# An attention, MLP and MoE kernel: attention units in another order, fewer weight tiles converted ahead of the MLP

## The chip, the cores and the metric

The kernel runs on one core of a Trainium2 chip. A core has TensorE (PE, matmul), VectorE (DVE), ScalarE (ACT), GpSimd (POOL) and SyncE (SP, which issues DMAs). Each engine works through its own instructions in the order in which the program lists them, and waits on semaphores for the others. The time is that of one execution on the device, in microseconds (us). The median of three runs of the kernel before is 1107.69 us (1107.59 to 1109.96).

## The reference

Three stages in a row, all in float32 (in outline):

```python
# 1: recurrent attention, 4 batches x 8 heads x 768 steps, head width 48
state = alpha[:, :, t, :, None] * state + einsum('bhd,bhe->bhde', k[:, :, t], v[:, :, t])
y[:, :, t] = einsum('bhd,bhde->bhe', q[:, :, t], state)
# 2: MLP on x = y as [3072 tokens, 384]; w_in [384, 2048], w_out [2048, 384]
h = x @ w_in;  g = h * sigmoid(h);  x = g @ w_out
# 3: noisy top-2 mixture of 8 experts, each 384 -> 1024 -> 384 with relu
logits = x @ w_gate + log1p(exp(x @ w_noise)) * noise;  two best experts per token
out[token] += weight * (relu(x @ w1[e]) @ w2[e])
```

The weights of the MLP come in as 64-bit floats and are used as float32 in two parts, a high part h and a rest l.

## The kernel before

**Attention** is cut into 24 chunks of 128 steps (6 for each batch). For a chunk c, `prep_a`, `prep_b` and `prep_c` make running products of alpha (two scans on DVE, P and R), q times P (POOL, L221), and k times R (DVE, L230). Then come the units on PE: `unit_kt` transposes k (copied to SBUF by ACT as kts), `unit_a` multiplies k with q (16 matmuls), DVE masks the product (`am`, L258), `unit_kv` multiplies kts with v, DVE makes the next state S from it (L277, L278), `unit_y` makes y from S and the masked product in two halves, ACT copies y out as xr, and `unit_x` transposes it to the layout that the MLP reads; ACT and DVE make its high part xh and its rest xl (L310, L311). Three chunks make a token block of 384.

**The MLP** takes 8 blocks, each in 16 steps m. In a step `l1` makes 128 rows of h in nine matmuls (three for each third of the width: two parts of x, two of w_in). `act1` makes the tanh (ACT, L484), gf (DVE, L487), its high part gh (ACT, L492) and the rest gl (DVE, L494). `l2` of two steps earlier adds nine matmuls of g with w_out to three accumulators (L504).

**Weight conversion.** `conv` turns one of the 32 weight tiles (16 of w_in, "i", and 16 of w_out, "o") into its two parts. Three DVE instructions (`narrow`, L148 to L150) make a float32 tile f from the 64-bit words; ACT writes h (L383); POOL issues a DMA that adds h onto f in SBUF (L386, the accumulate); ACT writes l from what is left (L387). A tile of w_out also goes through `fold`: PE transposes f three times (L94), ACT copies that (ft, L394), and `product` multiplies it with the gate's weights (L399), so that the gate's columns come out of `l2` as well; those 16 columns are split too (L401 to L403). f turns over a ring of six buffers (wf and row in the profile are its two tiles), the raw words over three (wraw): the load of a tile is issued on SP once the tile three before it has been narrowed.

**What sets the order.** The program is in the order in which it is written; nothing reorders it. `later(n, fn)` puts a piece of work off until n calls of `tick` have passed. Here it is used for the parts of `conv`, and, in the prologue and in block 0, for am, S and xl as well, one tick later. `stage1_units` hands out attention units one at a time, five to a chunk. The prologue runs 16 of them with nine conversions between them, three chunks in all and the head (`unit_kt`, `unit_a`) of the fourth; block 0 then runs one unit and two conversions in each step until the 32 tiles are through, the first conversion and a tick ahead of the step's tanh, the second after it. From block 1 on nothing is put off.

Of the kernel before, what the change touches and what calls it, by code (L numbers as in the profile page):

```python
# [8 lines left out]
F32 = mybir.dt.float32  # L9
# [43 lines left out]
def attention_mlp_moe(ctx: ExitStack, tc: tile.TileContext, aqk, vt, win, wout, wgn, noise, w12,  # L53
# [175 lines left out]
        k = aqk_t[c][2]  # L229
        DVE.tensor_tensor(k, k, R[:, :, 1:], OP.mult)  # L230

    def bank(c, name, n):
        if c < CPB:
            return pa.tile([128, 512], F32, name=name)[:, :n]
        return p1.tile([128, 512], F32, name="ps1")[:, :n]

    def unit_kt(c):
        t = aqk_t[c]
        if c % NCB < NCB - 1:
            p = bank(c, "acc0", NP * PR).rearrange("p (a b) -> p a b", a=NP)  # L240
            for i in range(NP):
                flip(p[:, i], t[2][:, i])
            k = s1.tile([C, NP, PR], F32, name="kts")
            KTs[c] = k
            ACT.activation(k, p, AF.Copy)

    def unit_a(c):
        t = aqk_t[c]
        p = [p1.tile([C, NP, C], F32, name="ps1") for _ in range(2)]
        for pr in range(NP):  # L250
            for s in range(2):
                PE.matmul(p[s][:, pr], t[2][s * 64:s * 64 + D, pr], t[1][s * 64:s * 64 + D, pr],  # L252
                          start=True, stop=True)

        def am():
            for s in range(2):
                a = s1.tile([C, NP, C], F32, name="am", bufs=3)
                DVE.tensor_tensor(a, p[s], mask_b, OP.mult)  # L258
                AM[c, s] = a

        later(1, am)

    def unit_kv(c):
        if c % NCB == NCB - 1:
            return
        p = p1.tile([PR, NP, 2 * D], F32, name="ps1")
        k = KTs.pop(c)
        for i in range(NP):
            PE.matmul(p[:, i], k[:, i], v_t[c][:, 2 * i:2 * i + 2], start=True, stop=True)
        def state():  # L270
            s = s1.tile([PR, NP, 2 * D], F32, name="S")
            pcm = pcm_t.pop(c)
            if c % NCB == 0:
                DVE.tensor_tensor(s, p, pcm, OP.mult)
            else:
                tmp = s1.tile([PR, NP, 2 * D], F32, name="St", bufs=1)
                DVE.tensor_tensor(tmp, p, Sst[c - 1], OP.add)  # L277
                DVE.tensor_tensor(s, tmp, pcm, OP.mult)  # L278
            Sst[c] = s

        later(1, state)

    def unit_y(c, g):
        t = aqk_t[c]
        if g == 0:
            y_t[c] = bank(c, "acc1", DM).rearrange("p (a b) -> p a b", a=H)
        y = y_t[c]
        for pr in (2 * g, 2 * g + 1):
            f = c % NCB == 0
            if not f:  # L290
                PE.matmul(y[:, 2 * pr:2 * pr + 2], t[1][:, pr], Sst[c - 1][:, pr],
                          start=True, stop=False)
            for s in range(2):
                h = 2 * pr + s
                PE.matmul(y[:, h], AM[c, s][:, pr], v_t[c][:, h], start=f, stop=f or s == 1)  # L295
        if g == 1:
            x = s1.tile([C, KD, 128], F32, name="xr", bufs=1)
            ACT.activation(x.rearrange("p a b -> p (a b)"), y.rearrange("p a b -> p (a b)"), AF.Copy)
            y_t[c] = x

    def unit_x(c):
        j, cc = divmod(c, CPB)
        if cc == 0:
            XH[j], XL[j] = x_tiles(BT)
        x = y_t.pop(c)
        p = bank(c, "acc2", DM).rearrange("p (a b) -> p a b", a=KD)
        for k in range(KD):
            flip(p[:, k], x[:, k])
        sl = slice(cc * C, (cc + 1) * C)
        ACT.activation(XH[j][:, :, sl], p, AF.Copy)  # L310
        later(1, lambda: DVE.tensor_sub(XL[j][:, :, sl], p, XH[j][:, :, sl].bitcast(F32)))  # L311

    dq, lazy, clock = [], [True], [0]

    def later(n, fn, pe=0):
        if lazy[0]:
            dq.append((clock[0] + n, pe, fn))
        else:
            fn()

# [4 lines left out]
        for *_, fn in sorted(due, key=lambda x: x[1]):  # L325
            fn()

    def head(c):
        unit_kt(c)
        unit_a(c)  # L330

    def stage1_units():
        head(0)
        yield
        for c in range(NCH):
            nx = c + 1
            if nx + 1 < NCH and nx + 1 > 2:
                load_chunk(nx + 1)
            if nx < NCH:
                prep_a(nx)  # L340
            unit_kv(c)
            yield
            if nx < NCH:
                prep_b(nx)
            unit_y(c, 0)
            yield
            unit_y(c, 1)
            if nx < NCH:
                prep_c(nx)
            yield  # L350
            if nx < NCH:
                head(nx)
            yield
            unit_x(c)
            yield
# [3 lines left out]
    def unit():  # L359
        next(gen, None)  # L360

    order = [("i", 0), ("o", 0), ("i", 1), ("o", 1), ("o", 2), ("i", 2), ("o", 3), ("o", 4), ("o", 5)]
    for m in range(3, MF):
        order += [("i", m), ("o", m + 3)] if m + 3 < MF else [("i", m)]
    wloads, wpreps = list(order), list(order)

    def wl(n=1):
# [5 lines left out]
    def conv():  # L373
        if not wpreps:
            return
        kind, m = k = wpreps.pop(0)
        f = next_f()
        narrow(raw.pop(k), f.bitcast(I32))
        wl()
        h, l = (win_h, win_l) if kind == "i" else (wo_h, wo_l)  # L380
        h, l = [x[:, m].rearrange("p k j -> p (k j)") if kind == "i" else x[:, m, :DM] for x in (h, l)]
        o = kind == "o"
        later(1, lambda: ACT.activation(h, f, AF.Copy, scale=-1.0))  # L383
        if o:
            later(1, lambda: fold(m, f), 1)
        later(2, lambda: POOL.dma_start(f, h.bitcast(F32), accum_op=OP.add))  # L386
        later(4, lambda: ACT.activation(l, f, AF.Copy, scale=-1.0))  # L387

    def fold(m, f):
# [22 lines left out]
    prep_c(0)  # L412
    nc.scalar.dma_start(wgn_t, wgn)
    nc.scalar.dma_start(nz, noise)
    conv()
    for i in range(16):
        tick()
        unit()
        if 0 < i < 15 and i % 5 in (1, 3, 0):
            conv()  # L420
    tick()

    def range_load(i):
        raw["r", i] = load_w(win if i < MF else wout, i % MF)
# [246 lines left out]
    for i in range(NS + LAG):  # L671
        if i < NS:
# [14 lines left out]
            if j == NB - 1:  # L687
# [17 lines left out]
                if 1 <= m < 9:  # L705
                    w3_split(0, m - 1)
            if j == 0:
                if held:
                    step(held[0])
                    step(held[0])  # L710
                conv()
                tick()
                ac = act1(j, m)
                step(ac)
                if held:
                    run(held.pop())
                held.append(ac)
                conv()
                tick()
            else:  # L720
                if held:
                    run(held.pop())
# [3 lines left out]
                run(act1(j, m))  # L726
            if m < MF - 1 and j < NB - 1:
                unit()
        if i >= LAG:
            j, m = divmod(i - LAG, MF)  # L730
            l2(j, m)
# [235 lines left out]
def step(gen):  # L967
    try:
        return next(gen)
    except StopIteration as end:  # L970
        return end.value
# [63 lines left out]
```

## Time and profile before

| | |
|---|---|
| median of three runs | 1107.69 us |
| the profiled execution | 1108.36 us, of which 1106.5 us from first to last instruction (its span) |
| PE busy | 1049.3 us, 95% |
| DVE, ACT, POOL busy | 587.3, 409.3, 239.1 us |
| mean granted clock of PE | 0.989 |
| slices 1 to 4 of 40 (27.7 us each), PE busy | 4, 6, 8 and 8 tenths; later 9 nearly throughout |

The times of the rows further down count from the start of the span. "Idle before, releaser" in a row is how long the engine stood still ahead of that instruction, and what it waited for. Busy time of PE hides how fast it works: the same nine matmuls of `l1` are found at two speeds. The first `l1` stands at 69.36 us, the first of block 1 at 156.95 us.

### The profile page before, as it was taken

The numbers are of one execution on the slowest core, as the hardware profiler recorded it, in microseconds if no ns is written. First come the engines' busy times: TensorE is split into PE (matmuls) and PEld (weight loads), VectorE is DVE, ScalarE is ACT, GpSimd is POOL, SyncE is SP. The second block draws the span as 40 slices with busy tenths as digits, with TensorE's granted clock in tenths as the row PEclk, the third lists the DMA queues.
The fourth block names the chain that finished last, engine by engine and source line by source line (L and its number), as shares of the span: only waits on it lengthen the run. The fifth ranks groups of instructions, "written<-read, shape, count | busy, mean of one in ns | idle before, by whom it ended". The sixth has DMA issues, their size and how long they took to land.

```text
span 1106.5 us, 16769 instructions
## 1 busy us (share of the span) xinstructions
PE 1049.3 (95%) x6323; PEld 1017.0 (92%) x6323; DVE 587.3 (53%) x1353; ACT 409.3 (37%) x885; POOL 239.1 (22%) x236
## 2 busy tenths in 40 slices
PE   4688999999999999999999998999999999999996
PEld 4588999899998999989999988999999999999996
DVE  6768856658677576775637442244333342423221
ACT  3446643334343333333334423234333233323221
POOL 4233210300313003130020222211212222121213
PEclk9999999999999999999999999999999999999999
DMA  7569962533324223250033333445444434353313
GB/s 207 147 149 223 229 182 90 186 109 126 119 84 147 87 75 119 76 149 17 1 98 101 98 129 61 103 95 151 119 90 95 104 73 116 81 119 83 49 12 49
DMA packets 56121, 120.30 MB, mean 109 GB/s; under 512 B 7024, under 2 KB 34544, under 8 KB 56032
## 3 DMA queue, kind: packets, MB, share of 16 engines
q1 hardware_dynamic: 39744, 91.60, 27.4%
q0 software_dynamic: 15872, 26.97, 13.8%
q8 instruction: 52, 0.85, 0.3%
q10 hardware_dynamic: 416, 0.58, 0.2%
q14 instruction: 37, 0.30, 0.1%
HBM read 82.22 MB, written 30.61 MB: 102 GB/s over the span
## 4 chain that ended last, share of the span: by engine, by line
issue 38%; PE 36%; DMA 12%; DVE 6%; POOL 5%; ACT 2%; POOLq 0%; ACTq 0%; DVEq 0%
PE acc L504 12%; DMA out_dram<-y,xrow 12%; PE ph L477 11%; POOL xd L611 3%; PE acc L787 3%; PE ph L761 3%; PE ps L252 2%; PE ps L295 1%; PE ps L94 1%; POOL out_dram L799 1%; DVE P L209 1%; PE ps L399 1%; PE acc L295 1%; POOL aqk L221 1%; DVE gf L487 1%
## 5 line engine op out<-in xcount | busy, mean ns | idle before, releaser
L787 PE MATMUL acc<-w3h,hx 128*128 128x384 f32 x832 | 241.1, 341 | 1.3 <-ACT y L797 1.3
L768 DVE SCALAR_TENSOR_TENSOR hx<-ph,hx 128x64 fp32r<-128x64 f32 (+1 forms) x192 | 79.2, 443 | 288.7 <-ACT hx L764 278.0
L799 POOL DMA_INDIRECT out_dram<-y,xrow x64 | 99.1, 1549 | 347.7 <-ACT y L797 285.1
L764 ACT ACTIVATE hx<-ph 128x448 fp32r<-128x448 f32 (+1 forms) x128 | 65.5, 518 | 262.9 <-PE ph L761 176.9
L787 PEld LDWEIGHTS acc<-w3h,hx 128*128 128x128 f32 x832 | 152.7, 188 | 4.8 <-ACT y L797 1.6
L787 PE MATMUL acc<-w3l,hx 128*128 128x384 f32 x448 | 149.9, 335 | 0.0
L504 PE MATMUL acc<-wo_h,gh 128*128 128x400 f32 x384 | 142.9, 372 | 0.0
L761 PE MATMUL ph<-xh,w3h 128*128 128x384 f32 (+1 forms) x384 | 136.1, 354 | 3.9 <-ACT hx L764 3.9
L761 PE MATMUL ph<-xh,w3l 128*128 128x384 f32 (+1 forms) x384 | 135.1, 352 | 0.0
L761 PE MATMUL ph<-xl,w3h 128*128 128x384 f32 (+1 forms) x384 | 134.9, 351 | 0.0
L504 PE MATMUL acc<-wo_h,gl 128*128 128x400 f32 x384 | 133.9, 349 | 0.0
L504 PE MATMUL acc<-wo_l,gh 128*128 128x400 f32 x384 | 133.6, 348 | 0.0
L477 PE MATMUL ph<-xh,win_h 128*128 128x384 f32 x384 | 132.1, 344 | 0.0
L477 PE MATMUL ph<-xl,win_h 128*128 128x384 f32 x384 | 130.6, 340 | 0.0
L477 PE MATMUL ph<-xh,win_l 128*128 128x384 f32 x384 | 130.5, 340 | 0.0
L484 ACT ACTIVATE th<-ph 128x384 f32<-128x384 f32 x128 | 62.8, 491 | 176.3 <-PE ph L477 170.3
L487 DVE SCALAR_TENSOR_TENSOR gf<-th,ph 128x384 f32<-128x384 f32 x128 | 70.4, 550 | 88.9 <-ACT th L484 84.5
L494 DVE TENSOR_TENSOR gl<-gf,gh 128x384 fp32r<-128x384 f32 x128 | 79.2, 618 | 69.3 <-ACT gh L492 66.8
L492 ACT ACTIVATE gh<-gf 128x384 fp32r<-128x384 f32 x128 | 67.1, 525 | 117.8 <-DVE gf L487 113.1
L787 PEld LDWEIGHTS acc<-w3l,hx 128*128 128x128 f32 x448 | 80.8, 180 | 0.7
L761 PEld LDWEIGHTS ph<-xh,w3h 128*128 128x128 f32 x384 | 72.5, 189 | 7.2 <-ACT hx L764 4.2
L761 PEld LDWEIGHTS ph<-xh,w3l 128*128 128x128 f32 x384 | 72.5, 189 | 3.6
(166 smaller groups left out, 1738.1 us busy)
## 6 DMA issues: line engine op xcount, KB each, us to landing
wraw<-in_w_dram SPq DMA_DIRECT2D x64, 384.0 KB, 4.5
aqk<-in_aqk_dram SPq DMA_DIRECT2D x23, 674.2 KB, 8.5
wraw<-in_win_dram SPq DMA_DIRECT2D x32, 384.0 KB, 3.6
wraw<-in_wout_dram SPq DMA_DIRECT2D x32, 384.0 KB, 3.3
xrow<-xd SPq DMA_DIRECT2D x48, 196.5 KB, 2.6
xd<-pad SPq DMA_DIRECT2D x8, 589.5 KB, 8.4
v<-in_v_dram SPq DMA_DIRECT2D x24, 192.0 KB, 5.4
out_dram<-pad SPq DMA_DIRECT2D x2, 1344.0 KB
```

Source lines behind the costliest of these rows:

```text
L477: PE.matmul(p, w[:, m, k], x[:, k], start=(n == 0), stop=(n == 3 * KD - 1))
L484: ACT.activation(th, p, AF.Tanh, scale=-0.5)
L487: DVE.scalar_tensor_tensor(g, th, 1.0, p, op0=OP.add, op1=OP.mult)
L492: ACT.activation(gh, g, AF.Copy)
L494: DVE.tensor_tensor(gl, g, gh.bitcast(F32), OP.subtract)
L504: PE.matmul(ACC[j][i], g[:, sl], w[:, m], start=(m == 0 and n == 0), stop=(m == MF - 1 and n == 2))
L611: st = POOL.indirect_dma_start(out=xd, out_offset=bass.IndirectOffsetOnAxis(ap=idx[:, i, k:k + 1], axis=0), in_=r[:, i, :RW], in_offset=No ...
L761: PE.matmul(p[:, :N], w[:, k, fs], x[:, k], start=(n == 0), stop=(n == 3 * KD - 1))
L764: ACT.activation(hx[:, :N], p[:, :N], AF.Relu)
L768: DVE.scalar_tensor_tensor(hx[:, o:o + b - a], p[:, a:b], 0.0, hx[:, a:b].bitcast(F32), op0=OP.max, op1=OP.subtract)
L787: PE.matmul(AC3[e, g][t][:m], hx[:, o:o + m], w[:, f], start=(f == 0 and q == 0), stop=(f == FF - 1 and q == len(prods) - 1))
L799: st = POOL.indirect_dma_start(out=out, out_offset=bass.IndirectOffsetOnAxis(ap=x[:n, RW - 1:].bitcast(I32), axis=0), in_=y[a:a + n], in_o ...
```

## The change

It has five parts. The units of a chunk come as `unit_kt` with `unit_a`, `unit_kv`, `unit_y` in two, `unit_x`, with no head of the next chunk ahead of `unit_x`; the prologue ends with the third chunk, after 15 units. In the prologue am, S and xl are no longer put off (`soon`); from block 0 on they are. The prologue converts four tiles, i0, i1, i2 and o0, at units 0, 1, 6 and 11, and the order of tiles is then i3, o1, i4, o2 and so on, two in each of 14 steps of block 0. `fold` and the accumulate of an o tile both come two ticks after its narrowing, the fold first. In a step of block 0 the tanh comes last, behind both conversions and the unit. Beside this the PSUM banks of the first three chunks come from the pool p1 (three banks in turn) and no longer from pa.

```diff
-    def bank(c, name, n):
-        if c < CPB:
-            return pa.tile([128, 512], F32, name=name)[:, :n]
-        return p1.tile([128, 512], F32, name="ps1")[:, :n]
...
-        later(1, am)
+        soon(am)
...
-        later(1, state)
+        soon(state)
...
-        later(1, lambda: DVE.tensor_sub(XL[j][:, :, sl], p, XH[j][:, :, sl].bitcast(F32)))
+        soon(lambda: DVE.tensor_sub(XL[j][:, :, sl], p, XH[j][:, :, sl].bitcast(F32)))
-    dq, lazy, clock = [], [True], [0]
+    dq, lazy, clock = [], [False], [0]
     def later(n, fn, pe=0):
+        dq.append((clock[0] + n, pe, fn))
+    def soon(fn):
         if lazy[0]:
-            dq.append((clock[0] + n, pe, fn))
+            later(1, fn)
         else:
             fn()
...
     def stage1_units():
-        head(0)
-        yield
         for c in range(NCH):
             nx = c + 1
             if nx + 1 < NCH and nx + 1 > 2:
                 load_chunk(nx + 1)
             if nx < NCH:
                 prep_a(nx)
-            unit_kv(c)
+            unit_kt(c)
+            unit_a(c)
             yield
             if nx < NCH:
                 prep_b(nx)
+            unit_kv(c)
+            yield
             unit_y(c, 0)
             yield
-            unit_y(c, 1)
             if nx < NCH:
                 prep_c(nx)
-            yield
-            if nx < NCH:
-                head(nx)
+            unit_y(c, 1)
             yield
             unit_x(c)
             yield
...
-    order = [("i", 0), ("o", 0), ("i", 1), ("o", 1), ("o", 2), ("i", 2), ("o", 3), ("o", 4), ("o", 5)]
-    for m in range(3, MF):
-        order += [("i", m), ("o", m + 3)] if m + 3 < MF else [("i", m)]
+    order = [("i", 0), ("i", 1), ("i", 2)]
+    for m in range(MF):
+        order += [("o", m)] + ([("i", m + 3)] if m + 3 < MF else [])
...
-        if o:
-            later(1, lambda: fold(m, f), 1)
-        later(2, lambda: POOL.dma_start(f, h.bitcast(F32), accum_op=OP.add))
+        if kind == "o":
+            later(2, lambda: fold(m, f), 1)
+        later(2, lambda: POOL.dma_start(f, h.bitcast(F32), accum_op=OP.add), 2)
...
-    conv()
-    for i in range(16):
+    for i in range(3 * 5):
+        unit()
         tick()
-        unit()
-        if 0 < i < 15 and i % 5 in (1, 3, 0):
+        if i in (0, 1, 6, 11):
             conv()
-    tick()
+    lazy[0] = True
...
             if j == 0:
+                conv()
+                tick()
                 if held:
                     step(held[0])
                     step(held[0])
                 conv()
                 tick()
-                ac = act1(j, m)
-                step(ac)
                 if held:
                     run(held.pop())
-                held.append(ac)
-                conv()
-                tick()
...
             if m < MF - 1 and j < NB - 1:
                 unit()
+            if j == 0:
+                held.append(act1(j, m))
+                step(held[0])
```

Three places show what moves. The first is PE in the prologue, from the end of `unit_a` of the second chunk to its first y (xr: transposes of `unit_x`; row, wf: transposes of `fold`; kts: `unit_kv`; S and am: `unit_y`). Before:

```order
L252 MATMUL ps_265<-aqk 128x128
L252 MATMUL ps_266<-aqk 128x128
L94 MATMUL acc_285<-ident,xr 128x128 x3
L94 MATMUL ps_298<-ident,row 128x128 x3
L269 MATMUL ps_316<-v,kts 112x96 x4
L94 MATMUL ps_333<-ident,wf_116 128x128 x3
L291 MATMUL acc_344<-S,aqk 128x96
L295 MATMUL acc_344<-v,am 128x48 x2
```

Now the same stretch reads:

```order
L247 MATMUL ps_268<-aqk 128x128
L247 MATMUL ps_269<-aqk 128x128
L264 MATMUL ps_288<-v,kts 112x96 x4
L286 MATMUL ps_302<-S,aqk 128x96
L290 MATMUL ps_302<-v,am 128x48 x2
```

The two folds have left the stretch, and `unit_x` of the chunk before has gone ahead of it.

The second place is DVE in the prologue around the masking of the second chunk (wf_116, row: narrowing of a weight tile; P and R: the scans of the next chunk). Before:

```order
L258 TENSOR_TENSOR am<-ps_265,mask 128x512
L258 TENSOR_TENSOR am<-ps_266,mask 128x512
L148 TENSOR_SCALAR row<-wraw 128x384
L149 SCALAR_TENSOR_TENSOR row<-wraw,row 128x384
L150 SCALAR_TENSOR_TENSOR row<-wraw,row 128x384
L403 TENSOR_TENSOR wo_l<-fp,wo_h 128x16
L311 TENSOR_TENSOR xl<-acc_285,xh 128x3x128
L209 SCALAR_TENSOR_TENSOR P<-aqk,past 112x516
L210 TENSOR_SCALAR past<-P 112x4
L211 RECIPROCAL past<-past 112x4
```

Now:

```order
L230 TENSOR_TENSOR aqk<-aqk,R 112x512
L306 TENSOR_TENSOR xl<-ps_242,xh 128x3x128
L209 SCALAR_TENSOR_TENSOR P<-aqk,past 112x516
L210 TENSOR_SCALAR past<-P 112x4
L211 RECIPROCAL past<-past 112x4
L253 TENSOR_TENSOR am<-ps_268,mask 128x512
L253 TENSOR_TENSOR am<-ps_269,mask 128x512
L219 SCALAR_TENSOR_TENSOR R<-aqk,past 112x516
L220 MEMSET past 112x4
L272 TENSOR_TENSOR St<-ps_288,S 112x384
```

The scan P of the next chunk now stands ahead of the masking, and no narrowing stands between the masking and the next state.

The third place is ACT in one step of block 0, from one tanh to the next (win_l, wo_l: the rests of weight tiles, which wait for an accumulate; win_h, wo_h: the high parts). Before:

```order
L387 ACTIVATE win_l<-row 128x384
L383 ACTIVATE wo_h<-wf_116 128x384
L394 ACTIVATE ft<-ps_699 128x384
L298 ACTIVATE xr<-ps_650 128x384
L492 ACTIVATE gh<-gf 128x384
L387 ACTIVATE wo_l<-wf_116 128x384
L401 ACTIVATE fp<-ps_694 128x16
L402 ACTIVATE wo_h<-fp 128x16
L383 ACTIVATE win_h<-row 128x384
L484 ACTIVATE th<-ph 128x384
```

Now:

```order
L378 ACTIVATE wo_l<-row 128x384
L374 ACTIVATE win_h<-wf_116 128x384
L385 ACTIVATE ft<-ps_618 128x384
L482 ACTIVATE gh<-gf 128x384
L378 ACTIVATE win_l<-wf_116 128x384
L392 ACTIVATE fp<-ps_613 128x16
L393 ACTIVATE wo_h<-fp 128x16
L374 ACTIVATE wo_h<-row 128x384
L293 ACTIVATE xr<-ps_574 128x384
L474 ACTIVATE th<-ph 128x384
```

The copy ft of a fold now belongs to a tile that was narrowed in the step before, and the rest of an o tile stands first in the step.

## Rows read from the trace of the kernel before

**Rows 1.** Stretches of the span: busy us of PE, PEld, DVE, ACT, POOL (count); clock, DMA
```profile
0.00:69.20 69.20, 44.89 (x232) 41.23 (x232) 43.61 (x79) 24.98 (x61) 23.11 (x37) 1.00 0.61 160
69.20:89.60 20.40, 16.71 (x90) 16.16 (x91) 19.14 (x39) 11.67 (x31) 7.62 (x9) 0.92 0.85 208
89.60:136.10 46.50, 42.86 (x290) 41.86 (x289) 39.30 (x86) 28.93 (x79) 14.48 (x17) 0.96 0.92 227
136.10:157.00 20.90, 20.90 (x140) 20.57 (x140) 11.56 (x21) 9.77 (x23) 3.90 (x5) 1.00 0.87 224
```
**Rows 2.** Waits of PE, 0 to 160 us: total us, times, longest
```profile
PE ps L94 <- DVE wf L150: 9.1, 3, 3.7
PE ps L94 <- DVE row L150: 6.4, 2, 3.6
```
**Rows 3.** The chain that ended last: nine matmuls of l1 at five steps
```profile
69.36 3.08 PE ph L477 x9
...
89.80 1.58 PE ph L477 x9
...
136.25 1.56 PE ph L477 x9
...
150.23 1.58 PE ph L477 x9
...
156.95 1.57 PE ph L477 x9
```
**Rows 4.** PE in order of time: start us, us, what, idle before
```profile
24.54 0.99 PE L94 MATMUL acc<-ident,aqk 112*128 112x112 f32 x4
25.45 2.08 PE L252 MATMUL ps<-aqk 48*128 48x128 f32 x16
27.46 0.90 PE L94 MATMUL acc<-ident,xr 128*128 128x128 f32 x3
...
31.12 1.67 PE L269 MATMUL ps<-v,kts 128*112 128x96 f32 x8
...
36.28 0.58 PE L291 MATMUL acc<-S,aqk 112*128 112x96 f32 x2
...
38.72 1.43 PE L399 MATMUL ps<-wgn_t,ft 128*128 128x16 f32 x6
...
41.78 0.98 PE L295 MATMUL acc<-v,am 128*128 128x48 f32 x4
```
**Rows 5.** DVE in order of time, second chunk of the prologue
```profile
27.57 1.29 DVE L258 TENSOR_TENSOR am<-ps,mask 128x512 f32<-128x512 f32 x2 [4.15 <-PE ps L252]
28.77 0.35 DVE L148 TENSOR_SCALAR row<-wraw 128x384 int32<-128x384 int32 x1
...
30.23 0.17 DVE L403 TENSOR_TENSOR wo_l<-fp,wo_h 128x16 fp32r<-128x16 f32 x1
...
30.78 1.22 DVE L209 TENSOR_TENSOR_SCAN P<-aqk,past 112x516 f32<-112x516 f32 x1
...
33.30 2.17 DVE L150 SCALAR_TENSOR_TENSOR wf<-wraw,wf 128x384 int32<-128x384 int32 x1
35.39 0.55 DVE L277 TENSOR_TENSOR St<-ps,S 112x384 f32<-112x384 f32 x1
...
36.45 1.22 DVE L219 TENSOR_TENSOR_SCAN R<-aqk,past 112x516 f32<-112x516 f32 x1
37.81 1.04 DVE L230 TENSOR_TENSOR aqk<-aqk,R 112x512 f32<-112x512 f32 x1
```
**Rows 6.** POOL in order of time: two accumulates of w_in tiles issued
```profile
71.69 0.86 POOL L386 DMA_DIRECT2D row<-win_h  x1 [6.30 <-ACT win_h L383]
...
140.42 0.86 POOL L386 DMA_DIRECT2D row<-win_h  x1 [2.95 <-ACT win_h L383]
```
**Rows 7.** ACT in order of time: the rests that wait for these two
```profile
77.82 0.52 ACT L387 ACTIVATE win_l<-row 128x384 fp32r<-128x384 f32 x1 [0.67 <-DMA row<-win_h]
...
143.42 0.53 ACT L387 ACTIVATE win_l<-row 128x384 fp32r<-128x384 f32 x1 [0.32 <-DMA row<-win_h]
```

More of the change, by code (lines that the diff above doesn't have):

```diff
@@ L239, in unit_kt @@
         if c % NCB < NCB - 1:
-            p = bank(c, "acc0", NP * PR).rearrange("p (a b) -> p a b", a=NP)
+            p = p1.tile([C, NP, PR], F32, name="ps1")
             for i in range(NP):
@@ L285, in unit_y @@
         if g == 0:
-            y_t[c] = bank(c, "acc1", DM).rearrange("p (a b) -> p a b", a=H)
+            y_t[c] = p1.tile([C, H, D], F32, name="ps1")
         y = y_t[c]
@@ L305, in unit_x @@
         x = y_t.pop(c)
-        p = bank(c, "acc2", DM).rearrange("p (a b) -> p a b", a=KD)
+        p = p1.tile([128, KD, C], F32, name="ps1")
         for k in range(KD):
@@ L326, in tick @@
             fn()
-    def head(c):
-        unit_kt(c)
-        unit_a(c)
     def stage1_units():
-        head(0)
-        yield
         for c in range(NCH):
@@ L381, in conv @@
         h, l = [x[:, m].rearrange("p k j -> p (k j)") if kind == "i" else x[:, m, :DM] for x in (h, l)]
-        o = kind == "o"
         later(1, lambda: ACT.activation(h, f, AF.Copy, scale=-1.0))
-        if o:
-            later(1, lambda: fold(m, f), 1)
-        later(2, lambda: POOL.dma_start(f, h.bitcast(F32), accum_op=OP.add))
+        if kind == "o":
+            later(2, lambda: fold(m, f), 1)
+        later(2, lambda: POOL.dma_start(f, h.bitcast(F32), accum_op=OP.add), 2)
         later(4, lambda: ACT.activation(l, f, AF.Copy, scale=-1.0))
```

## The prediction

> **What bounds the kernel now.** I read the share of each engine by stretch first. From 136 us on PE is busy without a gap, and the page's slices show 9 tenths nearly to the end; so what makes the first `l1` of block 1 start earlier is kept to the end, since PE's order behind it does not change in length. That `l1` stands at 156.95 us [rows 3]. All of the change lies ahead of it: a prologue of 69.2 us, in which PE is busy for 44.9, and block 0 of 87.6 us [rows 1, 3].
>
> Then the waits of PE: 15.5 us stand on the last narrowing instruction of a weight tile, ahead of the fold's transposes [rows 2]. The fold comes one tick after its tile was queued on DVE, and y is queued behind the fold on PE. The times of PE and DVE show the rest [rows 4, 5]: the second chunk's masking starts at 27.57 and its y only at 36.28, for between them DVE narrows two tiles (28.77 to 30.23 is one, 1.46 us; the second is stretched, with 2.17 for its last instruction), copies xl, scans P and makes the state. So the prologue is a chain through DVE's queue, with PE and DVE idle by turns.
>
> In block 0 the first three steps took (89.80 − 69.36) / 3 = 6.81 us each, the next eight (136.25 − 89.80) / 8 = 5.81, the last two, past all conversions, (156.95 − 150.23) / 2 = 3.36 [rows 3]. In the eight, PE is busy for 92%, DVE for 85%, and the DMA engines for 92% of the time [rows 1]: three resources near their end at once.
>
> **The prologue, worked out.** The masking, the state and xl follow their matmuls at once, folds leave the first two chunks, and five tiles go.
>
> *To unit_a of the second chunk.* The first chunk is as before up to its masking. P of the second chunk is now ahead of the masking; its data is there by 13.5 (an estimate: ACT reads it just after 13.7 now). Then on DVE: P with two small instructions 1.6, am 1.2, tile 1.46, R 1.36, S 0.55, tile 1.46 [rows 5]. POOL multiplies for the next state beside this second tile, and the stretched instruction shows what that costs: 2.17 for 0.56, so 1.6. Then k times R, 1.04 [rows 5]. From 13.5 that is 23.8. The transposes of k take 0.9, and `unit_a` starts at 24.7; before it was 25.45 [rows 4].
>
> *To unit_a of the third.* `unit_a` 2.1, to 26.8. am is out 1.3 later. But `unit_kv` needs kts from ACT, where the rest of i0 stands ahead; its accumulate is queued on POOL behind the product that waits for S, and so issued at about 21.5. With 3.0 us from issue to use (140.42 to 143.42 [rows 6, 7], the nearest calm stretch) ACT is free at 25, the two sums over the next alpha take until 27, kts 27.5, `unit_kv` 1.4: y starts at 28.9. y is 36.28 to 42.76 without one product of 1.23, 5.25 [rows 4]: 34.2. Copy 0.5, transposes 0.7, xh and xl 1.0: `unit_a` at 36.4.
>
> *To l1.* `unit_a` 2.1, with the masking hidden behind `unit_kv` 1.4, y 5.25: 45.2. The fold of o0 stands there with 0.7 (its tile was narrowed some 4 us earlier), then the transposes 0.7 and xh 0.5: **l1 starts at 47.1**, 22.3 earlier than 69.36. Bounds: 43 if POOL and ACT never come between (the chain of unit_a, masking, y and copies is 11 us a chunk), 53 if the accumulates need the 6.1 us of 71.69 to 77.82 [rows 6, 7] and DVE is stretched twice more.
>
> **Block 0, worked out.** 28 conversions instead of 23 makes 14 steps with two instead of eleven and a half. Per step the tiles, loads, accumulates and one unit are what the eight middle steps had; the head that the prologue no longer runs comes in, and the head of the seventh chunk goes out to block 1: nothing between them. What goes is the wait of the fold: it now reads a tile narrowed in the step before. In the eight steps one such wait was 2.6, and PE then worked at half rate for 3.4 us, 1.7 lost; without both a step is 5.81 − 4.3 / 8 = 5.27. The DMA share of 92% in 5.81 gives 5.35 as a floor. I take **5.6**, halfway between floor and row, because three full queues seldom fit without a gap: 78.4 us. Bounds: 5.27, and 6.81, the first three steps.
>
> The last two steps: 6.7. The first step is at half rate: nine matmuls in 3.08 instead of 1.57 [rows 3], 1.5 more; what `unit_a` takes longer there is about what the missing `l2` saves. `l1` of block 1 then starts at 47.1 + 78.4 + 6.7 + 1.5 = **133.7**, 23.2 us earlier.
>
> The tanh last in its step costs nothing by this sum: gf of step m is on DVE behind the first narrowing of step m + 1, and `l2` needs it a step later still; it takes away the waits of DVE for the tanh, which are on no chain here. The three turning banks of p1 make `unit_a` of a chunk wait for xl of the chunk before, which is in the chain above (the last 0.5). SP's loads keep three tiles ahead; the chunks' loads move by one tile in SP's queue and are needed two steps later: nothing. From block 1 on, where nothing is put off, only the place of the head differs, with a step or more to spare: nothing.
>
> The profiled execution took 1108.36 us, 1.86 outside its span and 0.7 above the median of the runs. 1108.36 − 23.2 = 1085.2, and I forecast **1085 us**.
>
> **Two rules.** Nine matmuls take 3.08 at 69.36 and 1.57 later: that is 1.2 and 2.4 GHz, though the clock column reads 1.00 up to there, and PE had worked 44.9 of 69.2 us before [rows 1, 3]. The Trainium skill (TensorE: Matmul & The Clock Gate, What's actually happening) says that a gate halves the array's clock after idleness and frees it after sustained work. By that rule a prologue with fewer gaps may reach the full clock sooner, the first rival below; by the rows it did not up to 69 us.
>
> An accumulate of 196,608 bytes took 6.1 us from issue to use in the loaded stretch and 3.0 later [rows 6, 7]. The Trainium skill (DMA: Bandwidth & Descriptors, Anatomy of one DMA — SWDGE (gpsimd) path) gives 2.0 us and the bytes over 436 GB/s, 2.45 us as an estimate. By the page the second and third rivals below would not exist and y would start 0.5 earlier; the rows have the queue in them, which the page's figure for one DMA has not.
>
> **The rivals.** *The clock rises in the prologue.* In the second and third chunk `unit_a`, y and the transposes, 8.1 us a chunk, go at up to double rate, and block 0 starts warm. For: PE has gaps of 1 to 2 us in this chain, where it had up to 3.7 [rows 2]. Against: at 69.36 it was still slow. The two chunks would lose 8 of 16 us; half of that and the 1.5 of the cold start is 5.5, and steps at 5.4 give another 2.8: 1077.
>
> *Accumulates take part of each step.* The fold is later, so is the accumulate of an o tile, and its rest now stands first in ACT's step, with win_h, ft, gh and the tanh queued behind it and gl, `l2` and the next narrowing waiting for those. With 6.2 a step (between 5.6 and 6.81) and a prologue 5 us longer: 1085.2 + 8.4 + 5 = 1098.6. For: DMA at 92%; against: only 0.67 and 0.32 were waited there so far.
>
> *The accumulate sets the pace.* From the transposes of a fold over the issue (0.86), the landing, three ACT copies of 0.5 and the product to the transposes two tiles on is the landing plus 3.0 us, in two steps. The kernel becomes slower once a step passes (156.95 − 47.1 − 6.7) / 14 = 7.4, with a landing over 11.7 us. At 13 a step is 8.0 and the end 1085.2 + 33.6 = 1118.8. The row has 6.1.
>
> *What is gained is given back*: the prologue ends early, but block 0 has the same transfers to make (61% of 69.2 us and 85, 92 and 87% of the next three stretches [rows 1] are 120 us of full DMA up to 157 us) and can't shrink. Against: that includes filling rows for block 1 past 130 us, and at 133.7 a share of 90% over all would do. 1107.
>
> **How the numbers follow.** Forecast 0.50 (its own range 1080 to 1091, from steps of 5.3 to 5.9 and a prologue of 46 to 49); clock 0.17; part of each step 0.20; pace 0.10; given back 0.03. What a measurement can tell from no change is about 0.2%, 2.2 us. Faster 0.87, same 0.03, slower 0.10. The range goes from 1075, the clock with steps at 5.27, to 1101, the second rival with 2.5 us more; beyond are pace, given back and the edges.
>
> **What would show it.** The first `l1` near 47 us and that of block 1 near 134; no wait of PE on L150; two conversions a step in 5.6 us; the nine matmuls of the first step still near 3.1. Wrong if `unit_kv` waits for kts past 29 in the second chunk, if ACT waits more than 1 us a step for accumulates, or if steps are over 6.2.

## The result and the profile after

The changed kernel takes 1092.06 us (median of 4 runs, 1090.75 to 1094.8) where the kernel before took 1108.1 on the same chip: a ratio of 0.9855 (95% interval 0.9833 to 0.9878). Measured again beside other runs it was 1092.17, 0.9834 (0.9803 to 0.9864). The forecast was 1085, with 1075 to 1101 as its range; the inner range, 1080 to 1091, is missed by one. So the sign came out, and of the size 16 us where 23 were forecast, but the time was gained at other places than the prediction said.

The profiled execution took 1090.75 us, with a span of 1089.0 (1106.5 before). First the stretches of the changed kernel, the prologue and block 0 as in [rows 1] (columns as there: busy us and count of PE, PEld, DVE, ACT, POOL; clock, DMA share, GB/s):

```profile
0.00:45.81 45.81, 31.50 (x161) 28.90 (x161) 30.86 (x57) 16.00 (x34) 16.03 (x32) 1.00 0.64 173
45.81:149.53 103.72, 90.57 (x565) 87.65 (x565) 79.12 (x159) 56.09 (x148) 31.07 (x37) 0.90 0.85 207
```

The prologue ends after 45.81 us (forecast 47.1, before 69.20). But block 0 takes 103.72 us, where the kernel before took 156.79 − 69.20 = 87.59 (both by PE's own instructions; the chain in [rows 3] enters them at 69.36 and 156.95), and its clock is 0.90 on the mean. Now long waits of PE, 46 to 160 us, in the changed kernel (us in total, times, longest):

```profile
PE ps L286 <- DVE St L272: 6.5, 2, 3.3
PE ps L247 <- ACT ft L385: 2.4, 2, 1.5
PE ps L94 <- DVE row L150: 1.0, 1, 1.0
```

The waits on L150 [rows 2] have nearly gone, as forecast; others have come. ACT waited in this stretch longest for one thing, the accumulates of w_out tiles. Changed kernel first, 46 to 160 us:

```profile
ACT wo_l L378 <- DMA row<-wo_h: 23.6, 13, 6.4
ACT ft L385 <- PE ps L94: 12.5, 6, 3.3
ACT win_l L378 <- DMA wf<-win_h: 5.3, 4, 1.7
```

And the kernel before, 69 to 160 us:

```profile
ACT wo_l L387 <- DMA wf<-wo_h: 1.7, 2, 1.6
ACT win_l L387 <- DMA row<-win_h: 1.0, 2, 0.7
```

From block 1 on it is the other way round: the kernel before waits for POOL's product of q and P (L221), the changed one doesn't. Before, 157 to 1107 us, then after, 160 to 1100 us, each view's longest wait (the one for hx is in both, 3.9 before):

```profile
PE ps L252 <- POOL aqk L221: 10.6, 5, 2.7
```

```profile
PE ph L751 <- ACT hx L754: 4.3, 1, 4.3
```

The table follows the gain through the program. A "tanh i" is the start of the tanh of step i of the MLP on ACT (steps 0 to 15 are block 0); all in us, each from one profiled execution.

| run | first `l1` | tanh 0 | tanh 14 | tanh 16 | tanh 48 | span |
|---|---|---|---|---|---|---|
| before | 69.20 | 72.46 | 151.91 | 158.61 | 298.80 | 1106.5 |
| after | 45.81 | 53.09 | 145.39 | 155.24 | 288.56 | 1089.0 |
| lead of after | 23.4 | 19.4 | 6.5 | 3.4 | 10.2 | 17.5 |

So 23.4 us are won in the prologue, 20 of them are lost in block 0, and 14.1 are won again from block 1 on.

### The profile page after: what moved, and what is told of

The parts are those of the page before. It is cut to its first block, busy times and chain, and to the rows that moved or that the text cites. A ratio compares the mean times of both kernels' runs of the same rounds, so it can differ in the third digit from the quotient of the medians.

```text
span 1089.0 us, 16767 instructions
## 1 busy us (share of the span) xinstructions
PE 1044.9 (96%) x6323; PEld 1012.7 (93%) x6323; DVE 584.1 (54%) x1353; ACT 409.0 (38%) x885; POOL 235.9 (22%) x236
## 3 DMA queue, kind: packets, MB, share of 16 engines
q0 software_dynamic: 15872, 26.97, 14.1%
## 4 chain that ended last, share of the span: by engine, by line
PE 59%; issue 21%; DMA 13%; DVE 3%; POOL 1%; ACT 1%; POOLq 0%; SPq 0%; DVEq 0%; ACTq 0%
PE acc L494 19%; PE ph L467 17%; DMA out_dram<-y,xrow 10%; PE acc L777 5%; PE ph L751 5%; PE ps L290 4%; PE ps L247 2%; PE ps L94 2%; PE ps L286 2%; DMA row<-wo_h 2%; PE ps L264 1%; POOL out_dram L789 1%; DVE gl L484 1%; DMA wraw<-in_w_dram 1%; DVE R L219 1%
## 5 line engine op out<-in xcount | busy, mean ns | idle before, releaser
L484 DVE TENSOR_TENSOR gl<-gf,gh 128x384 fp32r<-128x384 f32 x128 | 85.1, 665 | 84.1 <-ACT gh L482 83.5
L494 PEld LDWEIGHTS acc<-wo_l,gh 128*128 128x128 f32 x384 | 73.7, 192 | 2.4 <-DVE wo_l L394 2.4
## 6 DMA issues: line engine op xcount, KB each, us to landing
xd<-pad SPq DMA_DIRECT2D x8, 589.5 KB, 8.4
```

What stands on the lines that cost most here:

```text
L484: DVE.tensor_tensor(gl, g, gh.bitcast(F32), OP.subtract)
L494: PE.matmul(ACC[j][i], g[:, sl], w[:, m], start=(m == 0 and n == 0), stop=(m == MF - 1 and n == 2))
```

## The experiments

Theory A says that the accumulates pace block 0; rival B, that the load on the DMA engines does; theory C, that PE waits there for a PSUM bank; theory P, that the later gain is POOL's product of q with P, which no longer stands between scatters and `unit_a`. Each ratio is to the kernel before on the same chip.

**The rest of an o tile one tick later** (changed kernel):

```diff
-        later(4, lambda: ACT.activation(l, f, AF.Copy, scale=-1.0))
+        later(5 if kind == "o" else 4, lambda: ACT.activation(l, f, AF.Copy, scale=-1.0))
```

> The changed kernel with one edit: the rest (l) of an o tile is written five ticks after its narrowing instead of four, so that it stands behind the second conversion of ACT's step and no longer first in it. Nothing is left out. Theory A (block 0 is long because ACT, in order, waits for the accumulates of the o tiles, which are issued only after the later fold): ACT's waits on these accumulates, 17.3 us in the changed kernel, fall below 6, block 0 (first l1 to first l1 of block 1, 103.7 us now) gets 8 to 15 us shorter, time 1077 to 1084 us. Rival B (block 0 is set by the DMA engines, whose share is 85%): the waits move to another instruction and the time stays within 3 us of 1092. Rival C (it is set by the wait of y for the PSUM bank that the state holds, with DVE stretched by POOL): within 3 us too, with the two waits of 3.2 us still there.

Measured: 1087.68 us, ratio 0.9791 (0.9745 to 0.9837); tanh 16 at 151.99 (155.24). ACT's waits for rows of wo fall to one of 5.7 us, at the end, but block 0 gains only 3.3. Theory A's 8 to 15 us are missed: ACT now waits elsewhere, 18.0 us for PE ahead of ft and 5.9 for the rows of w_in. The intervals of this ratio and of the changed kernel's touch, so the time alone settles nothing.

**No accumulate at all** (changed kernel; the rests l are written as zeros, so the products with them add nothing; every other instruction is kept):

```diff
-        later(2, lambda: POOL.dma_start(f, h.bitcast(F32), accum_op=OP.add), 2)
-        later(4, lambda: ACT.activation(l, f, AF.Copy, scale=-1.0))
+        later(4, lambda: ACT.activation(l, f, AF.Copy, scale=0.0))
```

> The changed kernel without the accumulating DMAs: the rests of all weight tiles are written as zeros by the same ACT instruction, and POOL issues none of the 32 accumulates, so the low parts of the weights are left out of the result. Theory A: with nothing to wait for on ACT, block 0 falls from 103.7 to 85 to 88 us, time 1072 to 1076 us. Rival B (DMA engines): the same direction, since 28 transfers go, with the DMA share of block 0 falling from 85% to under 65%. Rival C (bank of the state, DVE stretched): block 0 stays above 98 us and the time above 1086.

Measured: 1078.85 us, ratio 0.9711 (0.9676 to 0.9746); tanh 16 at 140.39, 14.9 us earlier; tanh 0 to tanh 14 in steps of 5.77 us (6.59 in the changed kernel, 5.67 before). Its stretch of 46 to 150 us:

```profile
46.00:150.00 104.00, 99.32 (x646) 96.13 (x647) 84.71 (x177) 63.66 (x169) 7.98 (x11) 0.97 0.58 171
```

With the DMA share at 0.58 PE is busy for 95%. Leaving the accumulates out thus gives back 14.9 us, three quarters of the 20 lost. Whether their place in the order costs that, or their load on the DMA engines, this run can't tell, since theory A and rival B both foretold it; and what the kernel before would gain without them was not run.

**q times P early in the kernel before**: issued in `prep_a` from chunk 6 on, ahead of the scatters.

```diff
 # in prep_a
+        if c >= 6:
+            POOL.tensor_tensor(aqk_t[c][1], aqk_t[c][1], P[:, :, 1:], OP.mult)
 # in prep_b
-        POOL.tensor_tensor(q, q, P[:, :, 1:], OP.mult)
+        if c < 6:
+            POOL.tensor_tensor(q, q, P[:, :, 1:], OP.mult)
```

> The kernel before with one edit: from the seventh chunk on POOL's product of q and P is issued with prep_a, one unit earlier than now, so that it stands ahead of the route's six scatters on POOL. Theory P (most of the measured gain comes from blocks 1 to 6, where the new order of units gives that product two more units before unit_a needs it): the 10.6 us that PE waits on L221 fall below 3, and with the half clock behind each wait gone the time is 1093 to 1098 us, 10 to 15 us below before. Rival Q (the gain comes from the prologue and block 0): within 3 us of before, 1108.

Measured: 1097.22 us, ratio 0.9884 (0.9847 to 0.992); span 1090.7, 15.8 less, all of it behind tanh 16 (158.49). The traced execution is the fastest of four (1092.49); by the ratio the gain is about 13 us. The longest wait of PE, 157 to 1107 us:

```profile
PE ph L764 <- ACT hx L767: 3.8, 1, 3.8
```

The wait on L221 is gone, and with it what the changed kernel wins from block 1 on. How it arises is seen in the kernel before, POOL in order of time (start, us; L611 is a scatter of rows), and the first `unit_a` behind it on PE:

```profile
207.16 1.15 POOL L611 DMA_INDIRECT xd<-row,idx  x1 [2.15 <-DVE idx L606]
...
214.78 0.98 POOL L611 DMA_INDIRECT xd<-row,idx  x1 [0.30 <-issue]
215.77 1.19 POOL L221 TENSOR_TENSOR aqk<-aqk,P 112x512 f32<-112x512 f32 x1
```

```profile
217.02 1.16 PE L252 MATMUL ps<-aqk 48*128 48x128 f32 x16 [2.66 <-POOL aqk L221]
...
220.94 0.52 PE L477 MATMUL ph<-xh,win_h 128*128 128x384 f32 x1
...
222.11 0.33 PE L477 MATMUL ph<-xl,win_h 128*128 128x384 f32 x1
```

Six scatters hold POOL's queue for 8.6 us, the product stands behind them, and PE waits 2.66 and then works at 0.52 us a matmul, instead of 0.33 from 222.11 on. The wait comes once in each of five blocks. Behind three of them (2.66, 2.08 and 2.23 us) PE works at the lower rate for some ten matmuls; behind the two of 1.83 it doesn't.

**q times P late in the changed kernel**: the same edit the other way, the product moved from `prep_b` to `prep_c`, from chunk 6 on.

> The changed kernel with one edit: from the seventh chunk on POOL's product of q and P is issued with prep_c, two units later than now, which leaves it the two units before unit_a that it had in the kernel before. Theory P: PE waits on that product again, 8 to 12 us in all, and the time is 1103 to 1108 us, most of the gain gone. Rival Q: within 3 us of 1092.

Measured: 1087.93 us, ratio 0.9785 (0.9744 to 0.9827), no wait on L221; not slower. My expectation was wrong: it counted the units between the product and `unit_a`. What counts is how many steps lie between the scatters, which come at a fixed step of a block, and the next `unit_a`: two in the kernel before, five after the change, and five in this run as well, since the edit leaves `unit_a` where it was. In both the product stands behind the last scatter (at 212.13 in the changed kernel, scatters from 203.35; at 212.32 here), and `unit_a` comes only 9 us later (221.94 and 221.33).

**S at once** (changed kernel):

```diff
-        soon(state)
+        state()
```

> The changed kernel, but S (L272) is never put off: DVE reads kv's bank right behind kv's matmuls, in block 0 too. Theory C (a bank held too long): in the changed kernel y waited twice for S (6.5 us in two waits, 3.29 and 3.22), since y is the third user of three banks and S stood one tick behind. Then both waits go, the tanh of step 16 comes 4 to 6.5 us earlier (near 150 in place of 155.2), and the time is 3 to 6 us shorter (1086 to 1089 in place of 1092.06). Rival A (the accumulates alone set the pace of block 0): PE waits as long for something else, mostly the conversion's own parts; tanh 16 within 1.5 us of 155.2, time within 2 us of 1092.

Measured: 1089.05 us, ratio 0.9782 (0.9741 to 0.9822); tanh 16 at 157.0, not earlier. PE's waits for S, 46 to 160 us:

```profile
PE ps L286 <- DVE St L272: 2.5, 2, 2.0
```

4.0 us of bank waits went, and ACT still waits 24.6 us for rows of wo. PE stood still for less of block 0 (8.2 us, 13.2 in the changed kernel), but was busy for longer (97.22 us, 90.57), at a granted clock of 0.87 in place of 0.90. So in this trace the bank did not set the pace. The times don't put theory C out altogether: 1089.05 is next to its 1086 to 1089, and the traced execution is the slowest of the four (1091.32).

**The fold ahead of its accumulate again** (changed kernel):

```diff
-            later(2, lambda: fold(m, f), 1)
+            later(1, lambda: fold(m, f), 1)
```

> The changed kernel, but the fold is put back to one tick after its tile's start, so that its PE work stands ahead of the issue of its accumulate; nothing else. Theory A/C (putting the fold off took one wait away and uncovered others): block 0 gets a wait of PE for ACT's ft or fp back, 1 to 3.7 us each as in the kernel before (3.68 at 80.87, 2.63 at 110.98), but the bank's wait behind it (6.5) shrinks by about as much; tanh 16 within 2 us of 155.2, time 1090 to 1094. Rival F (the later fold is where the gain is): tanh 16 at 160 or later, time 1097 or more.

Measured: 1081.9 us, ratio 0.9737 (0.97 to 0.9774): about 10 us less than the changed kernel, and neither theory had said so. tanh 16 comes at 147.0 although the first `l1` is 2.3 later (48.13). In 46 to 160 us ACT no longer has a wait for rows of wo among its longer ones:

```profile
ACT ft L385 <- PE ps L94: 12.1, 12, 2.9
ACT wo_h L374 <- DVE row L150: 10.7, 10, 3.1
```

The reason is what the accumulate waits for. It overwrites the tile that the fold reads, so POOL can issue it only when PE has transposed that tile. Changed kernel, PE, POOL and ACT in order of time (the folds and accumulates of the tiles o4 and o5, with the rests of o4 and o5):

```profile
74.96 0.53 PE L94 MATMUL ps<-ident,row 128*128 128x128 f32 x3
...
79.45 0.53 PE L94 MATMUL ps<-ident,row 128*128 128x128 f32 x3
```

```profile
76.02 0.86 POOL L377 DMA_DIRECT2D row<-wo_h  x1 [3.53 <-ACT ft L385]
...
80.51 0.86 POOL L377 DMA_DIRECT2D row<-wo_h  x1 [2.73 <-ACT wo_l L378]
```

```profile
75.52 0.49 ACT L385 ACTIVATE ft<-ps 128x384 f32<-128x384 f32 x1 [0.79 <-PE ps L94]
...
79.81 0.52 ACT L378 ACTIVATE wo_l<-row 128x384 fp32r<-128x384 f32 x1 [1.48 <-DMA row<-wo_h]
80.65 0.47 ACT L385 ACTIVATE ft<-ps 128x384 f32<-128x384 f32 x1
...
88.85 0.52 ACT L378 ACTIVATE wo_l<-row 128x384 fp32r<-128x384 f32 x1 [3.80 <-DMA row<-wo_h]
```

The rows name ft as what POOL waited for at 76.02, but at 80.51 POOL issues before ft has begun (80.65). What fits them all is PE: the issue follows the end of the transposes by 0.53 to 0.56 us in fifteen of the sixteen o tiles. PE comes to the fold in its own order, so a fold one tick later puts the accumulate off, while the rest wo_l keeps its place on ACT, four ticks after the narrowing. ACT then meets the row unfinished, and win_h, ft and gh stand behind it. The chain that ended last runs through three of these accumulates, 21.5 us in all (start, us):

```profile
80.51 8.32 DMA row<-wo_h
...
110.29 4.52 DMA row<-wo_h
...
143.58 8.63 DMA row<-wo_h
```

Behind each of the first two it goes on over wo_l, win_h, ft and gh on ACT to gl on DVE, and through DVE's queue back to PE. The changed kernel once more, further down, has three of them in its chain as well (6.58, 3.64 and 9.12 us); with the fold a tick earlier the chain from 46 to 147 us has none. There POOL and ACT read:

```profile
67.23 0.85 POOL L377 DMA_DIRECT2D row<-wo_h  x1 [0.89 <-ACT ft L385]
```

```profile
74.23 0.53 ACT L378 ACTIVATE wo_l<-row 128x384 fp32r<-128x384 f32 x1
```

The rest of the tile issued at 67.23 now has 7.0 us until its place on ACT comes, and waits for nothing; in the changed kernel the tile issued at 80.51 was used at 88.85, as soon as it had landed. The transfers are the same in both, so the order alone brings this gain, and the load on the DMA engines by itself (a share of 0.85 and 0.86 in block 0) does not explain it. Of the 8.2 us by which tanh 16 is earlier, 3.8 come between tanh 14 and tanh 16: the last accumulate goes out at 135.23, ahead of the fills of the next experiment (136.13). From tanh 0 to tanh 14 it takes 86.35 us, 92.30 in the changed kernel and 88.81 in the run with the rest one tick later: ACT's waits for the rows explain a good half of that part, and what the remainder is stays open. From the second o tile to the sixteenth, an accumulate went out every 6.36 us in the changed kernel and every 5.84 here.

**The fills of xd later** (changed kernel; filling rows that block 1's scatters write over, 589.5 KB each):

```diff
-            if MF <= i < MF + E:
-                init_rows(i - MF)
+            if MF + 6 <= i < MF + 10:
+                init_rows(2 * (i - MF - 6))
+                init_rows(2 * (i - MF - 6) + 1)
```

> The changed kernel, but the eight fills of xd (589.5 KB each, SP, L177) are issued two a step from the seventh step of block 1 on in place of one a step from its first; SP then issues them behind a load that is itself late (168.39 in the changed kernel), not at 129.7 and 139.3. Theory G (the end of block 0 is late because the last accumulates lie behind those fills): ACT's wait for the last row of wo (6.36 us, 145.86 to 152.23) falls under 3 us, tanh 16 comes 3 to 6 us earlier, and the time is 2 to 5 us shorter (1087 to 1090). Rival H (the wait is the accumulate's own and only moves): tanh 16 within 1.5 us of 155.2; or what is gained at 155 is lost when scatters near 205 wait for the fills, time within 2 us of 1092 or longer.

Measured: 1085.38 us, ratio 0.9758 (0.9719 to 0.9796); tanh 16 at 150.03, 5.2 earlier, 3.8 of it behind tanh 14. Theory G holds. In the changed kernel SP issued five fills at once, and ACT then waited for the last row of wo, whose accumulate had gone out at 143.58 (SP, then ACT):

```profile
139.34 4.45 SPq L177 DMA_DIRECT2D xd<-pad  x5
```

```profile
152.23 0.52 ACT L378 ACTIVATE wo_l<-row 128x384 fp32r<-128x384 f32 x1 [6.36 <-DMA row<-wo_h]
```

With the fills at 164.17 that wait is 0.88:

```profile
145.38 0.53 ACT L378 ACTIVATE wo_l<-row 128x384 fp32r<-128x384 f32 x1 [0.88 <-DMA row<-wo_h]
```

**The tanh between the two conversions** (changed kernel):

```diff
+                ac = act1(j, m)
+                step(ac)
                 conv()
                 tick()
                 if held:
                     run(held.pop())
...
-                held.append(act1(j, m))
-                step(held[0])
+                held.append(ac)
```

> The changed kernel, but in block 0 the tanh stands between the two conversions of a step, as in the kernel before, and not at its end. Theory A (ACT rests because rows of wo come late, so that what stands behind a late row is late too): with the tanh ahead of the second conversion it is not held up by that conversion's late row; DVE's waits for gh (13.3 us in block 0 of the changed kernel) change by less than 4 us, and the time is within 3 us of 1092. Rival T (the place of the tanh is worth what the change brought): time longer by 5 us or more, PE waits for ACT's gh or DVE's gl in block 0.

Measured: 1088.99 us, ratio 0.9809 (0.9771 to 0.9847), tanh 16 at 152.59. DVE's waits for gh up to 150 us: 15.4 us, 17.0 in the changed kernel. The place of the tanh is worth nothing that these intervals show.

**The changed kernel once more**, beside the last three runs.

> The changed kernel itself, unedited, beside the other three on the same chip, so that they can be set against it and not only against the kernel before. Ratio to the kernel before near 0.9855, as it was measured (0.9833 to 0.9878), or a little lower where this chip gives the kernel before a longer time; its time 1087 to 1094.

Measured: 1092.17 us (1088.7 to 1094.68, 6 runs), 0.9834 (0.9803 to 0.9864); tanh 16 at 155.36, span 1088.8: its block 0 comes out the same.

**Early fold and late fills together** (both edits above).

> The changed kernel with two edits together: the fold one tick after its tile's start (as in the run with the fold before its accumulate) and the eight fills of xd two a step from the seventh step of block 1. Theory F2 (the fold reads the row of wo into which the accumulate writes, so the accumulate can only be issued behind the fold's flips; putting the fold off put the accumulate off, and with it the low part that ACT makes of the row): tanh 16 at 147 or earlier, no wait of ACT for a row of wo in block 0, time 1078 to 1082, that is 1 to 4 us less than with the fold alone (1081.9) if the fills still delay the end of block 0. Rival H2 (with the fold early, nothing in block 0 waits for the queue any more): time within 1 us of 1081.9, or longer because the fills then lie beside block 1.

Measured: 1085.83 us (1079.37 to 1087.45), ratio 0.9762 (0.9728 to 0.9796). Rival H2: nothing is won on top of the early fold. In its profile tanh 14 comes at 146.22, 5.3 later than with the early fold alone (140.91), from steps around 100 us, before any fill of either run; so executions of one program differ in block 0 by several us.

**Both, with the fold early in block 0 only.**

```diff
-            later(2, lambda: fold(m, f), 1)
+            later(1 if lazy[0] else 2, lambda: fold(m, f), 1)
```

> As the run with both edits, but the fold is early only in block 0; the one tile of wo that starts in the prologue keeps the later fold. In the run with the fold alone the first l1 came at 48.13 in place of 45.81. Theory: that 2.3 us came from the early fold in the prologue; the first l1 comes back to 46, and the time is 1 to 2.5 us below that of the run with both edits. Rival: the two start points meet again at the first step that DVE or the queue paces, and the time is the same within 1 us.

Measured: 1082.2 us (1078.58 to 1084.86), ratio 0.9741 (0.9711 to 0.9771). The first `l1` is back at 45.75; tanh 0 to tanh 16 takes 94.17 us (102.15 in the changed kernel). The time can't be told from that of the early fold alone, nor from the run with both edits. The versions with the early fold, here and by itself, are the fastest in which nothing is left out, and beat the changed kernel by about 10 us (by 6 with both edits).

**The late fold in the kernel before** (fold and accumulate both two ticks after, the fold first):

```diff
-            later(1, lambda: fold(m, f), 1)
-        later(2, lambda: POOL.dma_start(f, h.bitcast(F32), accum_op=OP.add))
+            later(2, lambda: fold(m, f), 1)
+        later(2, lambda: POOL.dma_start(f, h.bitcast(F32), accum_op=OP.add), 2)
```

> The kernel before, with the fold put off one tick and the accumulate ordered behind it, as the change does, and nothing else. Theory F2 (putting the fold off is a loss by itself): ACT's waits for rows of wo grow, block 0 is longer by 3 to 8 us, and so is the time (1111 to 1117 on a chip where the kernel before takes 1108 to 1111). Rival (as forecast: the fold's waits, 3.68 and 2.63 us, go): tanh 16 earlier by 3 to 6 us and the time 2 to 5 us shorter.

Measured: 1100.54 us, ratio 0.9909 (0.9879 to 0.9939), clearly shorter, though by less than 2%: the rival had the direction, but neither the size nor the place. The first `l1` comes 8.5 us earlier (60.70) and the span is 10.1 shorter; tanh 0 to tanh 16 takes 86.46 us, 86.15 before. In the prologue PE waited for narrowed tiles, 13.4 us in five waits before and 5.4 in three here; from 30 us on (kernel before, then this run; PE in order of time):

```profile
30.45 0.87 PE L94 MATMUL ps<-ident,row 128*128 128x128 f32 x3 [2.09 <-DVE wo_l L403]
35.62 0.88 PE L94 MATMUL ps<-ident,wf 128*128 128x128 f32 x3 [2.82 <-DVE wf L150]
49.74 0.87 PE L94 MATMUL ps<-ident,wf 128*128 128x128 f32 x3 [2.09 <-DVE wo_l L403]
54.90 0.87 PE L94 MATMUL ps<-ident,row 128*128 128x128 f32 x3 [2.82 <-DVE row L150]
```

```profile
33.30 0.73 PE L94 MATMUL ps<-ident,wf 128*128 128x128 f32 x3 [2.19 <-DVE wo_l L403]
49.31 0.87 PE L94 MATMUL ps<-ident,row 128*128 128x128 f32 x3 [1.34 <-DVE wo_l L403]
```

In block 0 of this run ACT's waits for rows of wo grow from 1.7 to 14.4 us, and PE's for the fold fall: there the two cancel. So the later fold is a gain where many o tiles stand in the prologue, and a loss of 6 to 10 us where block 0 has the o tiles.

## Why the prediction came out near, and where it was wrong

*The prologue: right.* First `l1` at 45.81 (47.1). `unit_a` of the second chunk starts at 22.80 (24.7), its y at 26.99 (28.9), `unit_a` of the third at 34.39 (36.4). kts doesn't hold it past 29. The lead of 2 us is there from the first mark on. One term of it was mis-read: the 1.6 us for a narrowing stretched beside the product for the state came as 0.54 (L149 at 18.55 took 1.10 in place of 0.56); the stretched row at 33.30 stood beside q times P (POOL L221, 33.54), not beside that product (L224). The chain of the changed kernel shows the nine matmuls of `l1` at the first step and at the fourth:

```profile
45.81 3.52 PE ph L467 x9
...
67.49 1.56 PE ph L467 x9
```

They go at the lower of the two levels (1.2 GHz) first and at the higher later, as at [rows 3], so the clock did not rise in the prologue and that rival is out.

*Block 0: the mechanism that I made the second rival is what happened.* "Per step the tiles, loads, accumulates and one unit are what the eight middle steps had", and "I take 5.6": from the first `l1` to that of step 14 it took 94.5 us (45.81 to 140.34), where 78.4 + 1.5 were forecast, 14.6 more. Without accumulates the steps are 5.77, so the floor that I took as reachable was one without them. The step of the working that failed is "What goes is the wait of the fold": that wait went, but the accumulate, which must follow the fold's transposes, went back with it, and ACT's waits for rows of wo grew from 1.7 to 23.6 us. The sum had put them at nothing. The second rival says just this, with 6.2 us a step and a chance of 0.20; the steps came to 6.59 by the tanh, and its prologue 5 us longer did not come. Two of the three signs that the prediction named for being wrong came too: ACT waited 1.8 us a step for accumulates (28.9 us over 16 steps), and steps were over 6.2. The third rival, in which each accumulate waits for the one before, is not what the rows show: in 6 of 15 cases an accumulate went out before the rest of the tile ahead of it was written.

*The last two steps: wrong by 2.5 up to `l1`, and by more behind it.* 6.7 forecast, 9.19 measured (140.34 to 149.53); then tanh 16 stands another 5.71 behind that `l1`, 1.82 before, since ACT waits for the row behind the five fills. I set that `l1` as the mark, and it overstated the lead: 7.3 us there, 3.4 at its tanh.

*"From block 1 on … nothing": wrong, by 14.1 us in favour.* "PE is busy without a gap" was read off tenths in slices of 27.7 us. In that stretch PE waited 10.6 us in five waits, with a stretch at half rate behind three of them, which such slices hide. I said that the head has "a step or more to spare"; it had gained three steps' distance from the scatters, and that was the gain.

So the sum was off by −19.8 up to the end of block 0 (a lead of 23.2 forecast, 3.4 come) and by +14.1 behind it, which is 5.7 of the 7 us between 1085 and 1092; the rest is the profiled execution against the median. The two errors cancelled for the most part. That the total came out near is luck, and it confirms neither part.

What stays open: why executions of the early fold differ by 5 us in block 0; how much of the 14.9 us that the accumulates cost is their load; and whether q times P early with the late fold in the kernel before adds up (−15.8 and −10.1 in span); it wasn't run.

## What to carry to other kernels

When a piece of work is put off to hide its wait, follow what must come behind it: here an in-place accumulate could only start after the fold had read the tile, its user kept its place, and the chain then ran through three unfinished accumulates, which cost more than the wait. A releaser that a view names is inferred: hold it against several instances before a cause is built on it. A column of nines over wide slices is no proof that an engine never waits; list its waits for the whole span before a stretch is called unchanged. And set the mark of a gain at the engine that everything later passes through, not at the first matmul of the next block.

## What the runs showed of the hardware that was not expected

In block 0 of one run an accumulate of 192 KB took from 3.0 to 10.6 us from issue to landing. The 10.6 were those of a w_in tile, issued at 81.05 and used at 91.67; among the w_out tiles the longest (8.63) had five fills of 589.5 KB issued 4.2 us ahead of it, from another queue. In the changed kernel the last narrowing instruction took 2.79 us instead of 0.56 while POOL multiplied (1.84 us) beside it:

```profile
55.06 2.79 DVE L150 SCALAR_TENSOR_TENSOR row<-wraw,row 128x384 int32<-128x384 int32 x1
```

```profile
55.59 1.84 POOL L221 TENSOR_TENSOR aqk<-aqk,P 112x512 f32<-112x512 f32 x1
```

The forecast priced this in the prologue and not in block 0, where DVE was stretched beside POOL at 90.61 (1.97) and 123.28 (3.13, both gl) too. All three stand in the chain that ended last, some 6 us longer together than at 0.56 each.
